# Both feed-forwards in five token blocks instead of six, with a ring of 1536 places

## The chip, the cores and the metric

The kernel runs on one core of a Trainium2 chip. The core has a matrix engine (TensorE, PE in the profile, its weight loads PEld), a vector engine (DVE), an activation engine (ACT), a general engine (POOL) and an engine that here only issues DMA transfers (SP). On-chip data lies in SBUF; matmul results lie in eight PSUM banks of 512 fp32 columns each. The metric is the device time of one execution in microseconds. Before the change it was 864.6 us, the median of 3 runs (862.94 to 866.23).

## The reference, cut to what matters

```
x = dilated/windowed attention(q, k, v)   # 4 batches, 8 heads, 576 tokens, head size 64
                                          # heads 0-3: the last 32 keys; heads 4-7: every 4th of the last 128
x = x as 2304 tokens x 512
h = x @ moe_w_in                          # 512 -> 2048
x = (h * cos(h)) @ moe_w_out              # 2048 -> 512
h = max(x @ w1, x @ w2, x @ w3)           # 512 -> 768, three times
y = h @ w_out                             # 768 -> 512
```

Inputs and output are fp32.

## The kernel before, in words

**Precision.** The big products are made of three passes in the fp32r type: every operand is kept as a rounded half "hi" and a rest half "lo", and hi·hi, lo·hi and hi·lo are added in PSUM (`PASSES`). So one 128 x 128 block of weights costs three matmuls per block of tokens. A matmul has the weights as its stationary operand (128 columns, loaded anew for each matmul) and the tokens of the current block as its moving operand (320 to 512 columns).

**The attention** is cut into 48 units: a unit is one batch, one pair of heads and 192 queries. Per unit PE makes the scores (L254, or L257 for the first 12 units), DVE adds the mask and takes the maximum (L261, into a tile `e`), ACT takes the exponential (L203), DVE or POOL normalizes (L293), PE transposes (L301), ACT or DVE copies (`pt`, L138) and PE multiplies with the values (L312). DVE then writes hi and lo of the result into the **ring** (L326, L328), the SBUF store from which the first feed-forward reads its tokens. In the ring of 1152 places a batch lies at place `b % 2 * 576`.

**The first feed-forward (FF1)** walks over six blocks of tokens (`BLOCKS1`, 512, 320, 320, 448, 320 and 384 tokens). A block has 16 steps, one for each 128 of the 2048 hidden columns. A step has 12 matmuls `h` (L342), the evaluation of h·cos(h) on DVE and ACT (kk L358 or L356, r L362, clamp L365, sine L203, product L374, halves L138/L134 and L376), and 12 matmuls that add the step of three steps before (`LAG = 3`) to four accumulator banks (L385). The `h` results take turns in two PSUM banks, so the `h` of step s+2 waits until the product of step s (L374) has read its bank. At the end of a block the four accumulators are copied to tiles `o` (L398, L400) and sent to a DRAM tensor x1d. These tiles have a pool of their own with two buffers (`osp`).

**The order of attention and FF1.** The 12 units of batch 0 come first, with the loads of the first weights. The units that a later block needs are run during the block before it: `plan[t]` lists the units that block t needs in addition, and `enter` spreads them over the first `LAST[t]` steps of the block before. With the six blocks these are 12 units ahead of FF1, and then 10, 2, 12, 8, 4 and 0 units during blocks 0 to 5. The pieces of a unit are put between the matmul groups of a step. Block 0 also converts the 32 FF1 weight tiles from 64-bit words to fp32 (ACT L175, DVE L181 and L184) and splits them into halves (L138, L194).

**The second feed-forward (FF2)** also has six blocks (`BLOCKS2`, 512, 320, 320, 512, 320, 320) with 6 steps each; a step has 36 matmuls (L342) for the three products, two maxima on DVE, and 12 accumulating matmuls (L385). Its tokens come back from x1d by batch (`x1_raw`) and are split into the ring (`x1_split`, L415, L416); the first batch is split during the last FF1 block. Its 24 weight tiles are loaded during the last FF1 block, as FF1 weight slots come free, and converted during that block and the first FF2 block.

**What sets the order.** The framework places the instructions of each engine with a scheduler of its own, by priority (about the order of the program text) and by estimated times; the order in the text is not always the order on the engine. All DMA transfers are issued in order by SP. `RUNS` is the number of SBUF tiles for loaded q/k/v groups: the load for unit n + RUNS is issued when unit n is done (`att_done`). The pool `tmp` (4 buffers) holds kk, r and the maxima, `sp` (4) holds the tiles `e`.

Of the kernel before, what the change touches and what calls it, by code (L numbers as in the profile page):

```python
# [8 lines left out]
F32 = mybir.dt.float32  # L9
F32R = mybir.dt.float32r  # L10
# [8 lines left out]
B, H, S, D = 4, 8, 576, 64  # L19
# [10 lines left out]
NC = DM // 128  # L30
NF1 = FF1 // 128
NF2 = FF2 // 128

BLOCKS1 = [512, 320, 320, 448, 320, 384]
BLOCKS2 = [512, 320, 320, 512, 320, 320]
TB = max(BLOCKS1 + BLOCKS2)
NBT = len(BLOCKS1)
RING = 2 * S
LAG = 3
RUNS = 6  # L40
KEYS = 2 * QB + WIN
START = (3, 6, 7)
STARTS1 = [sum(BLOCKS1[:n]) for n in range(len(BLOCKS1))]
STARTS2 = [sum(BLOCKS2[:n]) for n in range(len(BLOCKS2))]
WSLOTS = 2 * NF1

INV2PI = 1.0 / (2.0 * math.pi)
# [15 lines left out]
}  # L63


LAST = (13, 7, 10, 7, 8)
GROUP = (2, 1, 1, 1, 1, 1)

START_WEIGHTS = (0, 0, 2, 1, 0, 0, 0, 1, 0, 0, 1, 0, 1, 0, 1)
STEP_WEIGHTS = (  # L70
# [9 lines left out]
def token_runs(pair, i):  # L80

    if pair < 2:
        return [(0, 2 * QB, 2 * QB * i, 1)]
    out = []
    p, end = 2 * QB * i, 2 * QB * (i + 1)
    while p < end:
        r, t = divmod(p, S // 4)
        n = min(end - p, S // 4 - t)
        out.append((p - 2 * QB * i, n, 4 * t + r, 4))
        p += n  # L90
    return out
# [3 lines left out]
def body(  # L95
# [11 lines left out]
    nc = tc.nc  # L107
    pool = lambda name, bufs, **kw: ctx.enter_context(tc.tile_pool(name=name, bufs=bufs, **kw))
# [2 lines left out]
    wx = pool("wx", 2)  # L111
    xp = pool("xp", 1)
    ip = pool("ip", RUNS)
    tmp = pool("tmp", 4)
    gp = pool("gp", 2)
    sp = pool("sp", 4)
    ptp = pool("ptp", 2)
    smp = pool("smp", 8)
    osp = pool("osp", 2)
    drp = pool("drp", 1, space=bass.MemoryType.DRAM)  # L120
    ps = pool("ps", 1, space=PSUM)

# [23 lines left out]
    bank = [ps.tile([128, 512], F32, name=f"bank{n}") for n in range(8)]  # L146
    acc = bank[:4]
    h_bank = bank[4:6]
    a_bank = bank[6:]
# [156 lines left out]
    def att_out(u):  # L306
        b, p, i = u
        pt = st.pop(u)
        vs = given.pop(u)
        o = bank[places.pop(u)[1]]  # L310
        for j, h in HEADS:
            nc.tensor.matmul(  # L312
                o[64 * h : 64 * h + 64, j * QB : (j + 1) * QB],
                vs[j][2][:, 64 * h : 64 * h + 64],
                pt[:, 2 * j + h, :],
                start=True,
                stop=True,
            )
        x = ring[p]
        at = b % 2 * S  # L320
        parts = [
            (o[:, o0 : o0 + n], slice(at + t0, at + t0 + step * (n - 1) + 1, step))
            for o0, n, t0, step in token_runs(p, i)
        ]
        for ov, cols in parts:
            nc.vector.tensor_copy(x[:, 0, cols], ov)  # L326
        for ov, cols in parts:
            nc.vector.tensor_tensor(  # L328
                out=x[:, 1, cols], in0=ov, in1=x[:, 0, cols].bitcast(F32), op=ALU.subtract
            )  # L330


    g = {}
    PASSES = ((0, 0), (1, 0), (0, 1))

    def h_chunks(hv, w, t0, n_tok):

        c0 = t0 % RING

        def chunk(n, c):  # L340
            for j, (a, x) in enumerate(PASSES):
                nc.tensor.matmul(  # L342
                    hv,
                    w[:, a, 128 * c : 128 * c + 128],
                    ring[c][:, x, c0 : c0 + n_tok],
                    start=n == 0 and j == 0,
                    stop=n == NC - 1 and j == 2,
                )

        return chunk  # L350
# [30 lines left out]
    def acc_chunk(dst, t0, first, last, w, gt, dm):  # L381
        n_tok = gt.shape[-1]
        a_dm = acc[dm][:, :n_tok]
        for n, (a, x) in enumerate(PASSES):
            nc.tensor.matmul(  # L385
                a_dm,
                w[:, a, 128 * dm : 128 * dm + 128],
                gt[:, x, :],
                start=first and n == 0,
                stop=last and n == 2,  # L390
            )
        if last:
            if dst is x1d:
                o = osp.tile([128, TB], F32, tag="o", name="o")[:, :n_tok]
            else:
                o = ip.tile([128, TB], F32, tag="qkv", name="o")[:, :n_tok]
            if dm % 2:
                nc.vector.tensor_copy(o, a_dm)  # L398
            else:
                nc.scalar.copy(o, a_dm)  # L400
            nc.sync.dma_start(out=dst[dm, :, t0 : t0 + n_tok], in_=o)
# [1 line left out]

    x1raw = {}

    def x1_raw(b, c):
        raw = ip.tile([128, S], F32, tag="qkv", name="x1raw")
        nc.sync.dma_start(out=raw, in_=x1d[c, :, b * S : (b + 1) * S])
        x1raw[b, c] = raw

    def x1_split(b, c):
        raw = x1raw.pop((b, c))
        at = b % 2 * S
        hi, lo = (ring[c][:, x, at : at + S] for x in range(2))
        nc.scalar.copy(hi, raw)  # L415
        nc.vector.tensor_tensor(out=lo, in0=raw, in1=hi.bitcast(F32), op=ALU.subtract)  # L416

# [2 lines left out]
    def ff2_h(s):  # L420
        t, f = divmod(s, NF2)
        m = None
        for j in range(3):
            hv = (h_bank + a_bank)[flip[0] % 4][:, : BLOCKS2[t]]
            flip[0] += 1
            chunk = h_chunks(hv, halves[(j, f)], STARTS2[t], BLOCKS2[t])
            for n in range(NC):
                chunk(n, n)
            if j == 0:
                m = tmp.tile([128, TB], F32, tag="r", name="mx")[:, : BLOCKS2[t]]  # L430
                nc.vector.tensor_copy(m, hv)  # L431
            else:
                nc.vector.tensor_tensor(out=m, in0=hv, in1=m, op=ALU.max)  # L433
        gt = gp.tile([128, 2, TB], F32R, tag="g", name="gt")[:, :, : BLOCKS2[t]]
        nc.scalar.copy(gt[:, 0, :], m)  # L435
        nc.vector.tensor_tensor(
            out=gt[:, 1, :], in0=m, in1=gt[:, 0, :].bitcast(F32), op=ALU.subtract
        )
        g[s] = gt

    def ff2_acc(s):
        t, f = divmod(s, NF2)
        for dm in range(NC):
            acc_chunk(outT, STARTS2[t], f == 0, f == NF2 - 1, halves[("o", f)], g[s], dm)


    list1 = [("in", f) for f in range(LAG)]
# [34 lines left out]
    for t in range(NBT):  # L482
        us = []
        for b in range(B):
            n_tok = min(STARTS1[t] + BLOCKS1[t] - b * S, S)
            if n_tok > 0:
                us += units(b, dil, range(3)) + units(b, plain, range(-(-n_tok // (2 * QB))))
        plan.append([u for u in us if u not in sum(plan, [])])
# [47 lines left out]
    for s in range(NS + LAG):  # L536
# [16 lines left out]
        t, f = divmod(s, NF1)  # L553
        if s < NS:

            hv = (bank[3] if s == 2 else h_bank[(s + (s > 2)) % 2])[:, : BLOCKS1[t]]
            hc = h_chunks(hv, halves[("in", f)], STARTS1[t], BLOCKS1[t])
            chunks += [("h", n, c) for n, c in enumerate((2, 3, 0, 1))]
        if s >= LAG:
            chunks += [("a", dm, 0) for dm in range(NC)]  # L560
# [1 line left out]
        for j, (kind, x, c) in enumerate(chunks):  # L562
            if kind == "h":
                hc(x, c)
                if x == NC - 1:
                    hvs[s] = hv
                    ff1_reduce(s, hv)
            else:
                t0, f0 = divmod(s - LAG, NF1)
                acc_chunk(x1d, STARTS1[t0], f0 == 0, f0 == NF1 - 1, halves[("out", f0)], g[s - LAG], x)  # L570
            while done < len(pieces) and done * len(chunks) < (j + 1) * len(pieces):
                do, u = pieces[done]
                do(u)
                done += 1
            if j == 1:
                if s >= 1 and s - 1 < NS:
                    ff1_g(s - 1)
            if s < NF1:
                weights(STEP_WEIGHTS[s].count(j), WSLOTS)
# [3 lines left out]
            att_norm(to_norm, zt, tensor("norm"))  # L583
            to_out += to_norm
        to_norm = []
        if len(to_exp) >= GROUP[min(t, NBT - 1)] or (to_exp and s % NF1 >= LAST[min(t, 4)]):
            zt = att_exp(to_exp)
            to_norm, to_exp = to_exp, []
        k = s - (NS - NF1) - LAG - 1
# [6 lines left out]
            x1_split(0, k // 2 - 2)  # L596


    N2 = len(BLOCKS2) * NF2
    x1_at = {0: 1}  # L600
    for b in (2, 3):

        t = min(t for t in range(len(BLOCKS2)) if STARTS2[t] >= (b - 1) * S)
        x1_at[t * NF2] = b
    todo = []
    for s in range(N2 + 1):
        if s in x1_at:
            b = x1_at[s]
            todo += [(b, c) for c in range(NC)]
            for bc in todo[:2]:  # L610
                x1_raw(*bc)
        while at[3] < min(len(order), len(list1) + 4 * (s + 2)):
            weight_loads(1, len(order))
            weights(1, len(order))
        if s < N2:
            ff2_h(s)
        if s:
            ff2_acc(s - 1)
        if todo:
            x1_split(*todo.pop(0))  # L620
            if len(todo) >= 2:
                x1_raw(*todo[1])
# [79 lines left out]
```

## Time and profile before

| | |
|---|---|
| median of 3 runs | 864.6 us |
| the profiled execution | 862.63 us |
| its span, first to last instruction | 860.9 us |
| PE busy | 826.0 us, 96% |
| DVE busy | 541.2 us, 63% |
| ACT busy | 342.2 us, 40% |
| POOL busy | 107.0 us, 12% |
| granted TensorE clock, mean | 0.983 |

The busy time of PE is a union of records that overlap, since matmuls are pipelined: a matmul record lasts about 0.3 to 0.4 us, while the next one starts 0.15 to 0.23 us after it. What a matmul costs is therefore read from the distance between starts, or from the chain of waits, which gives a run of matmuls and the time that it took. A stage's cost is read from a table of windows whose edges are the first `h` matmul of each block.

### The profile page before, as it was taken

How to read it: one execution, taken by the hardware profiler on the slowest of the kernel's cores; microseconds unless marked ns; L12 is line 12 of the kernel's file. 1: busy time of each engine (PE TensorE's matmuls, PEld its weight loads, DVE VectorE, ACT ScalarE, POOL GpSimd, SP SyncE). 2: the span in 40 equal slices, each digit the busy share in tenths (PEclk: the TensorE clock that was granted, in tenths of full speed). 3: DMA queues.
4: the chain of work that ended last, by engine and by line, in shares of the span. 5: the costliest groups of instructions: out<-in, count | busy, mean ns of one | idle time of the engine just before them, and what ended most of it. 6: DMA issues, size and time to landing. Idle time of an engine off the chain costs nothing.

```text
span 860.9 us, 13231 instructions
## 1 busy us (share of the span) xinstructions
PE 826.0 (96%) x5030; PEld 734.5 (85%) x5030; DVE 541.2 (63%) x1466; ACT 342.2 (40%) x794; POOL 107.0 (12%) x104
## 2 busy tenths in 40 slices
PE   7858979999999999999999999999999999999998
PEld 6636657789988898889989999888899998889998
DVE  5989996566687877875676899982233333223232
ACT  6977857343278827832452445400011111001001
POOL 1654453110000000000000011210000000000000
PEclk9978999999999999999999999999999999999999
DMA  9972100110011211120110387100020201001000
GB/s 352 410 290 102 49 26 23 49 66 18 1 50 51 73 53 47 50 59 1 36 50 14 116 253 231 65 19 0 1 77 1 87 1 58 1 1 50 1 32 31
DMA packets 24400, 62.31 MB, mean 72 GB/s; under 512 B 2704, under 2 KB 7440, under 8 KB 24336
## 3 DMA queue, kind: packets, MB, share of 16 engines
q1 hardware_dynamic: 24336, 61.47, 20.9%
q8 instruction: 39, 0.64, 0.3%
q14 instruction: 25, 0.20, 0.1%
HBM read 52.02 MB, written 9.44 MB: 71 GB/s over the span
## 4 chain that ended last, share of the span: by engine, by line
PE 75%; DVE 11%; DMA 7%; ACT 3%; issue 2%; POOL 1%; SPq 0%; ACTq 0%; POOLq 0%; DVEq 0%
PE bank L342 42%; PE bank L385 26%; PE bank L254 3%; DMA w<-in_w_out 2%; DMA w<-in_w_in 2%; PE bank L312 2%; DVE wx L181 2%; DVE wx L184 2%; DMA x1d<-o 1%; PE bank L301 1%; ACT e L203 1%; DVE r L365 1%; DVE r L362 1%; DVE r L374 1%; DMA qkv<-in_qkv 1%
## 5 line engine op out<-in xcount | busy, mean ns | idle before, releaser
L342 PE MATMUL bank<-ring,w 128*128 128x320 f32 (+3 forms) x2448 | 471.1, 342 | 8.7 <-DVE r L374 7.7
L342 PEld LDWEIGHTS bank<-ring,w 128*128 128x128 f32 x2448 | 401.7, 189 | 42.1 <-DVE r L374 9.1
L385 PE MATMUL bank<-gt,w 128*128 128x320 f32 (+3 forms) x1584 | 314.0, 341 | 2.0 <-DVE gt L376 1.3
L385 PEld LDWEIGHTS bank<-gt,w 128*128 128x128 f32 x1584 | 262.0, 189 | 25.5 <-DVE gt L376 2.0
L203 ACT ACTIVATE r<-r,hpi 128x320 f32<-128x320 f32 (+3 forms) x96 | 59.2, 617 | 142.3 <-DVE r L365 141.9
L435 ACT CAST gt<-mx 128x320 fp32r<-128x320 f32 (+1 forms) x36 | 18.5, 514 | 226.5 <-DVE mx L433 226.5
L433 DVE TENSOR_TENSOR mx<-bank,mx 128x320 f32<-128x320 f32 (+1 forms) x72 | 40.1, 557 | 94.3 <-PE bank L342 94.3
L203 ACT ACT_TABLE_LOAD x58 | 74.4, 1283 | 18.5 <-DVE r L365 15.1
L203 ACT ACTIVATE e<-e,m 96x128 f32<-96x128 f32 x192 | 74.8, 391 | 7.1 <-DVE m L261 6.7
L194 POOL TENSOR_TENSOR w<-wx,w 128x512 fp32r<-128x512 f32 x44 | 60.7, 1388 | 123.2 <-DVE w L138 63.6
L374 DVE TENSOR_TENSOR r<-bank,r 128x320 f32<-128x320 f32 (+3 forms) x96 | 52.9, 552 | 23.7 <-ACT r L203 23.5
L431 DVE COPY mx<-bank 128x320 f32<-128x320 f32 (+1 forms) x36 | 20.1, 558 | 72.5 <-PE bank L342 72.5
L362 DVE SCALAR_TENSOR_TENSOR r<-kk,bank 128x320 f32<-128x320 int32 (+3 forms) x96 | 52.7, 549 | 9.6 <-ACT kk L356 7.9
L358 DVE TENSOR_SCALAR kk<-bank 128x320 int32<-128x320 f32 (+2 forms) x80 | 42.0, 525 | 26.5 <-PE bank L342 26.4
L261 DVE CUSTOM_DVE_ANT_0 e<-bank,cs 96x128 f32<-96x128 f32 x192 | 44.9, 282 | 14.8 <-PE bank L257 8.6
L134 POOL TENSOR_SCALAR gt<-r 128x320 fp32r<-128x320 f32 (+2 forms) x32 | 16.1, 503 | 288.1 <-PE bank L385 224.7
L376 DVE TENSOR_TENSOR gt<-r,gt 128x320 fp32r<-128x320 f32 (+3 forms) x81 | 42.7, 528 | 13.7 <-POOL gt L134 10.5
L184 DVE SCALAR_TENSOR_TENSOR wx<-w,wx 128x512 int32<-128x512 int32 x56 | 46.2, 828 | 0.3
L175 ACT ACTIVATE w<-w 128x512 f32<-128x512 f32 x56 | 36.4, 671 | 14.5 <-DMA w<-in_w 14.2
L254 PE MATMUL bank<-qkv 64*96 64x128 f32 x288 | 36.7, 299 | 3.7 <-DVE m L261 2.6
L365 DVE TENSOR_SCALAR r<-r 128x320 f32<-128x320 f32 (+3 forms) x96 | 39.4, 410 | 1.3
L254 PEld LDWEIGHTS bank<-qkv 64*96 64x96 f32 x288 | 25.3, 165 | 17.4 <-issue 6.3
(37 smaller groups left out, 509.4 us busy)
## 6 DMA issues: line engine op xcount, KB each, us to landing
qkv<-in_qkv SPq DMA_DIRECT2D x36, 336.0 KB, 2.9
w<-in_w SPq DMA_DIRECT2D x18, 512.0 KB, 4.5
w<-in_w_in SPq DMA_DIRECT2D x16, 512.0 KB, 9.4
w<-in_w_out SPq DMA_DIRECT2D x16, 512.0 KB, 10.0
qkv<-in_qkv SPq DMA_DIRECT2D x12, 432.0 KB, 9.3
x1raw<-x1d SPq DMA_DIRECT2D x16, 288.0 KB, 3.2
w<-in_w_o SPq DMA_DIRECT2D x6, 512.0 KB, 4.3
outT<-o SPq DMA_DIRECT2D x16, 160.0 KB, 1.8
```

Of the source, the lines that this page charges most:

```text
L184: nc.vector.scalar_tensor_tensor(out=x, in0=low, scalar=29, in1=x, op0=ALU.logical_shift_right, op1=ALU.bitwise_or)
L194: tensor("w_lo").tensor_tensor(out=w[:, 1, :], in0=x, in1=w[:, 0, :].bitcast(F32), op=ALU.subtract)
L203: last_table.append(nc.scalar.activation(*args, **kw).ins)
L254: nc.tensor.matmul(sv, q[rows], k[rows], start=True, stop=True)
L261: nc.vector.tensor_tensor_reduce(out=e[:, 2 * j + h, :], in0=places_of[j, h], in1=mask[:, kind, :], scale=-1.0 / math.sqrt(D), scalar=3e38 ...
L342: nc.tensor.matmul(hv, w[:, a, 128 * c : 128 * c + 128], ring[c][:, x, c0 : c0 + n_tok], start=n == 0 and j == 0, stop=n == NC - 1 and j == 2,
L358: nc.vector.tensor_scalar(out=kk.bitcast(I32), in0=hv, scalar1=INV2PI, scalar2=0.25, op0=ALU.mult, op1=ALU.add)
L362: nc.vector.scalar_tensor_tensor(out=r, in0=kk.bitcast(I32), scalar=-2.0 * math.pi, in1=hv, op0=ALU.mult, op1=ALU.add)
L365: nc.vector.tensor_scalar(out=r, in0=r, scalar1=ARG_HI, scalar2=ARG_LO, op0=ALU.min, op1=ALU.max)
L374: nc.vector.tensor_tensor(out=r, in0=hv, in1=r, op=ALU.mult)
L376: tensor("g_lo").tensor_tensor(out=gt[:, 1, :], in0=r, in1=gt[:, 0, :].bitcast(F32), op=ALU.subtract)
L385: nc.tensor.matmul(a_dm, w[:, a, 128 * dm : 128 * dm + 128], gt[:, x, :], start=first and n == 0, stop=last and n == 2,)
```

## The change

Both feed-forwards use one list of blocks, `BLOCKS = [512, 512, 512, 512, 256]`. A block of FF1 has 16 steps as before and a block of FF2 has 6. The ring has 1536 places, the first three blocks; a token t lies at place t % 1536, so a unit of batch 2 or 3 can cross the ring's end, and its copy into the ring is then cut in two (`parts`). FF2 no longer loads x1 by batch: it loads and splits it by block (`x1_raw(t, c)`, `x1_split(t, c)`), block t + 1 in the first steps of block t, at the places `AT2`. The plan of units follows from the blocks: 12 ahead of FF1, and then 12, 10, 12, 2 and 0 units during blocks 0 to 4, spread by the new `LAST`. The buffers: `tmp` has 5 (was 4) and also takes the tiles `o` of FF1, whose pool of two goes; `sp` has 3 (was 4), `RUNS` is 5 (was 6).

```diff
-BLOCKS1 = [512, 320, 320, 448, 320, 384]
-BLOCKS2 = [512, 320, 320, 512, 320, 320]
-RING = 2 * S
+BLOCKS = [512, 512, 512, 512, 256]
+RING = sum(BLOCKS[:3])
+AT2 = [RING - TB, 0, TB, RING - TB, 0]
-RUNS = 6
+RUNS = 5
-LAST = (13, 7, 10, 7, 8)
-GROUP = (2, 1, 1, 1, 1, 1)
+LAST = (13, 10, 12, 8)
+GROUP = (2, 1, 1, 1, 1)
...
-    tmp = pool("tmp", 4)
+    tmp = pool("tmp", 5)
-    sp = pool("sp", 4)
+    sp = pool("sp", 3)
-    osp = pool("osp", 2)
...
-        at = b % 2 * S
-        parts = [
-            (o[:, o0 : o0 + n], slice(at + t0, at + t0 + step * (n - 1) + 1, step))
-            for o0, n, t0, step in token_runs(p, i)
-        ]
+        parts = []
+        for o0, n, t0, step in token_runs(p, i):
+
+            while n:
+                at = (b * S + t0) % RING
+                k = min(n, (RING - at + step - 1) // step)
+                parts.append((o[:, o0 : o0 + k], slice(at, at + step * (k - 1) + 1, step)))
+                o0, n, t0 = o0 + k, n - k, t0 + step * k
...
-                o = osp.tile([128, TB], F32, tag="o", name="o")[:, :n_tok]
+                o = tmp.tile([128, TB], F32, tag="r", name="o")[:, :n_tok]
...
-    def x1_raw(b, c):
-        raw = ip.tile([128, S], F32, tag="qkv", name="x1raw")
-        nc.sync.dma_start(out=raw, in_=x1d[c, :, b * S : (b + 1) * S])
-        x1raw[b, c] = raw
+    def x1_raw(t, c):
+        raw = ip.tile([128, TB], F32, tag="qkv", name="x1raw")[:, : BLOCKS[t]]
+        nc.sync.dma_start(out=raw, in_=x1d[c, :, STARTS[t] : STARTS[t] + BLOCKS[t]])
+        x1raw[t, c] = raw
...
-            n_tok = min(STARTS1[t] + BLOCKS1[t] - b * S, S)
+            n_tok = min(STARTS[t] + BLOCKS[t] - b * S, S)
...
     for s in range(N2 + 1):
-        if s in x1_at:
-            b = x1_at[s]
-            todo += [(b, c) for c in range(NC)]
-            for bc in todo[:2]:
-                x1_raw(*bc)
+
+        if s % NF2 == 0 and s // NF2 + 1 < NBT:
+            todo += [(s // NF2 + 1, c) for c in range(NC)]
+            for key in todo[:2]:
+                x1_raw(*key)
```

## Rows read from the trace of the kernel before

**Rows 1.** The page: engines (section 1), then the chain of waits by engine.
```profile
PE 826.0 (96%) x5030; PEld 734.5 (85%) x5030; DVE 541.2 (63%) x1466; ACT 342.2 (40%) x794; POOL 107.0 (12%) x104
PE 75%; DVE 11%; DMA 7%; ACT 3%; issue 2%; POOL 1%; SPq 0%; ACTq 0%; POOLq 0%; DVEq 0%
```

**Rows 2.** Windows, edges at each FF1 block's first matmul and FF2's first two blocks.
```profile
core 0: us, PE busy (x) PEld busy (x) DVE busy (x) ACT busy (x) POOL busy (x), PEclk, DMA share, GB/s
22.74:171.08 148.34, 127.10 (x696) 93.44 (x695) 121.19 (x337) 103.49 (x256) 69.05 (x51) 0.92 0.36 134
171.08:234.76 63.68, 63.40 (x426) 59.98 (x425) 42.37 (x110) 21.01 (x45) 5.15 (x9) 1.00 0.09 29
234.76:320.13 85.37, 85.12 (x627) 74.82 (x626) 67.57 (x258) 58.06 (x143) 3.68 (x8) 1.00 0.19 57
320.13:412.79 92.66, 92.02 (x547) 79.73 (x546) 68.10 (x204) 46.81 (x105) 4.76 (x8) 1.00 0.12 37
412.79:480.63 67.84, 67.54 (x466) 63.41 (x465) 48.40 (x139) 32.29 (x70) 3.81 (x8) 1.00 0.11 33
480.63:557.52 76.89, 73.99 (x423) 71.57 (x422) 74.40 (x154) 36.87 (x66) 11.59 (x9) 1.00 0.57 180
557.52:620.12 62.60, 62.60 (x278) 51.84 (x277) 31.26 (x50) 4.21 (x7) 4.97 (x4) 1.00 0.04 13
```

**Rows 3.** The page, costliest groups: the two feed-forward matmul lines and L342's weight loads.
```profile
L342 PE MATMUL bank<-ring,w 128*128 128x320 f32 (+3 forms) x2448 | 471.1, 342 | 8.7 <-DVE r L374 7.7
L342 PEld LDWEIGHTS bank<-ring,w 128*128 128x128 f32 x2448 | 401.7, 189 | 42.1 <-DVE r L374 9.1
L385 PE MATMUL bank<-gt,w 128*128 128x320 f32 (+3 forms) x1584 | 314.0, 341 | 2.0 <-DVE gt L376 1.3
```

**Rows 4.** Chain of waits in time order: matmul runs at 512, 320, 448 columns; attention.
```profile
160.03 0.34 PE bank L301 x4
163.15 0.48 PE bank L312 x8
168.66 2.72 PE bank L385 x12
171.81 0.61 PE bank L254 x8
205.14 1.76 PE bank L385 x12
391.20 2.43 PE bank L385 x12
```

**Rows 5.** Timeline: start, duration; two groups at 384 columns; two weight loads after a wait.
```profile
513.51 2.24 PE L342 MATMUL bank<-ring,w 128*128 128x384 f32 x12
515.59 2.24 PE L385 MATMUL bank<-gt,w 128*128 128x384 f32 x12
...
27.49 0.30 PEld L342 LDWEIGHTS bank<-ring,w 128*128 128x128 f32 x2
```

**Rows 6.** DVE groups by shape (busy us, mean ns | idle before): L376 at three widths.
```profile
L376 DVE TENSOR_TENSOR gt<-r,gt 128x320 fp32r<-128x320 f32 x48 | 23.3, 485 | 8.3 <-POOL gt L134 6.7 <-ACT gt L138 1.6
L376 DVE TENSOR_TENSOR gt<-r,gt 128x448 fp32r<-128x448 f32 x16 | 10.0, 623 | 3.8 <-POOL gt L134 2.9 <-ACT gt L138 0.7
```

**Rows 7.** DVE groups by shape in the last FF1 block's window.
```profile
L181 DVE TENSOR_SCALAR wx<-w 128x512 int32<-128x512 int32 x18 | 12.6, 708 | 0.0
L358 DVE TENSOR_SCALAR kk<-bank 128x384 int32<-128x384 f32 x16 | 8.8, 548 | 0.9 <-PE bank L342 0.9
L365 DVE TENSOR_SCALAR r<-r 128x384 f32<-128x384 f32 x16 | 5.6, 350 | 0.0
```

**Rows 8.** Waits, whole span: who waited for whom, us in total, times, longest.
```profile
ACT o L400 <- DMA x1d<-o: 7.9, 3, 2.7
DVE o L398 <- DMA x1d<-o: 3.3, 4, 1.4
```

**Rows 9.** SP's waits, then its timeline at FF1 block 3's start.
```profile
SPq L217 <- PE bank L312: 241.9, 23, 49.9
...
336.59 0.33 SPq L217 DMA_DIRECT2D qkv<-in_qkv  x1
337.12 5.94 SPq L401 DMA_DIRECT2D x1d<-o  x4
344.69 0.33 SPq L217 DMA_DIRECT2D qkv<-in_qkv  x1
```

**Rows 10.** PE timeline in the start: scores (L257) and transposes (L301) of first units.
```profile
17.05 1.11 PE L257 MATMUL bank<-qkv 128*96 128x128 f32 x8
19.72 0.55 PE L301 MATMUL bank<-cs,e 96*128 96x96 f32 x4 [1.55 <-POOL e L293]
```

More of the change, by code (lines that the diff above doesn't have):

```diff
@@ L32 @@
 NF2 = FF2 // 128
-BLOCKS1 = [512, 320, 320, 448, 320, 384]
-BLOCKS2 = [512, 320, 320, 512, 320, 320]
-TB = max(BLOCKS1 + BLOCKS2)
-NBT = len(BLOCKS1)
-RING = 2 * S
+BLOCKS = [512, 512, 512, 512, 256]
+STARTS = [sum(BLOCKS[:n]) for n in range(len(BLOCKS))]
+TB = max(BLOCKS)
+NBT = len(BLOCKS)
+RING = sum(BLOCKS[:3])
+AT2 = [RING - TB, 0, TB, RING - TB, 0]
 LAG = 3
-RUNS = 6
+RUNS = 5
 KEYS = 2 * QB + WIN
 START = (3, 6, 7)
-STARTS1 = [sum(BLOCKS1[:n]) for n in range(len(BLOCKS1))]
-STARTS2 = [sum(BLOCKS2[:n]) for n in range(len(BLOCKS2))]
 WSLOTS = 2 * NF1
@@ L334, in body, with h_chunks @@
     PASSES = ((0, 0), (1, 0), (0, 1))
-    def h_chunks(hv, w, t0, n_tok):
-        c0 = t0 % RING
+    def h_chunks(hv, w, c0, n_tok):
         def chunk(n, c):
@@ L404, in body, with x1_split @@
     x1raw = {}
-    def x1_raw(b, c):
-        raw = ip.tile([128, S], F32, tag="qkv", name="x1raw")
-        nc.sync.dma_start(out=raw, in_=x1d[c, :, b * S : (b + 1) * S])
-        x1raw[b, c] = raw
[L411 to L414, printed above, removed]
+    def x1_raw(t, c):
+        raw = ip.tile([128, TB], F32, tag="qkv", name="x1raw")[:, : BLOCKS[t]]
+        nc.sync.dma_start(out=raw, in_=x1d[c, :, STARTS[t] : STARTS[t] + BLOCKS[t]])
+        x1raw[t, c] = raw
+    def x1_split(t, c):
+        raw = x1raw.pop((t, c))
+        hi, lo = (ring[c][:, x, AT2[t] : AT2[t] + BLOCKS[t]] for x in range(2))
         nc.scalar.copy(hi, raw)
@@ L423, in ff2_h @@
         for j in range(3):
-            hv = (h_bank + a_bank)[flip[0] % 4][:, : BLOCKS2[t]]
+            hv = (h_bank + a_bank)[flip[0] % 4][:, : BLOCKS[t]]
             flip[0] += 1
-            chunk = h_chunks(hv, halves[(j, f)], STARTS2[t], BLOCKS2[t])
+            chunk = h_chunks(hv, halves[(j, f)], AT2[t], BLOCKS[t])
             for n in range(NC):
@@ L429, in ff2_h @@
             if j == 0:
-                m = tmp.tile([128, TB], F32, tag="r", name="mx")[:, : BLOCKS2[t]]
+                m = tmp.tile([128, TB], F32, tag="r", name="mx")[:, : BLOCKS[t]]
                 nc.vector.tensor_copy(m, hv)
@@ L433, in ff2_h @@
                 nc.vector.tensor_tensor(out=m, in0=hv, in1=m, op=ALU.max)
-        gt = gp.tile([128, 2, TB], F32R, tag="g", name="gt")[:, :, : BLOCKS2[t]]
+        gt = gp.tile([128, 2, TB], F32R, tag="g", name="gt")[:, :, : BLOCKS[t]]
         nc.scalar.copy(gt[:, 0, :], m)
@@ L443, in ff2_acc @@
         for dm in range(NC):
-            acc_chunk(outT, STARTS2[t], f == 0, f == NF2 - 1, halves[("o", f)], g[s], dm)
+            acc_chunk(outT, STARTS[t], f == 0, f == NF2 - 1, halves[("o", f)], g[s], dm)
     list1 = [("in", f) for f in range(LAG)]
@@ L554, in body @@
         if s < NS:
-            hv = (bank[3] if s == 2 else h_bank[(s + (s > 2)) % 2])[:, : BLOCKS1[t]]
-            hc = h_chunks(hv, halves[("in", f)], STARTS1[t], BLOCKS1[t])
+            hv = (bank[3] if s == 2 else h_bank[(s + (s > 2)) % 2])[:, : BLOCKS[t]]
+            hc = h_chunks(hv, halves[("in", f)], STARTS[t] % RING, BLOCKS[t])
             chunks += [("h", n, c) for n, c in enumerate((2, 3, 0, 1))]
@@ L569, in body @@
                 t0, f0 = divmod(s - LAG, NF1)
-                acc_chunk(x1d, STARTS1[t0], f0 == 0, f0 == NF1 - 1, halves[("out", f0)], g[s - LAG], x)
+                acc_chunk(x1d, STARTS[t0], f0 == 0, f0 == NF1 - 1, halves[("out", f0)], g[s - LAG], x)
             while done < len(pieces) and done * len(chunks) < (j + 1) * len(pieces):
@@ L585, in body @@
         to_norm = []
-        if len(to_exp) >= GROUP[min(t, NBT - 1)] or (to_exp and s % NF1 >= LAST[min(t, 4)]):
+        if len(to_exp) >= GROUP[min(t, NBT - 1)] or (to_exp and s % NF1 >= LAST[min(t, len(LAST) - 1)]):
             zt = att_exp(to_exp)
@@ L596, in body @@
             x1_split(0, k // 2 - 2)
[L599 to L604, printed above, removed]
+    N2 = NBT * NF2
     todo = []
     for s in range(N2 + 1):
-        if s in x1_at:
-            b = x1_at[s]
-            todo += [(b, c) for c in range(NC)]
-            for bc in todo[:2]:
-                x1_raw(*bc)
+        if s % NF2 == 0 and s // NF2 + 1 < NBT:
+            todo += [(s // NF2 + 1, c) for c in range(NC)]
+            for key in todo[:2]:
+                x1_raw(*key)
         while at[3] < min(len(order), len(list1) + 4 * (s + 2)):
```

## The prediction

> **What bounds the kernel now.** I read the engines first: PE is busy for 96% of the span, the next engine for 63%, and the chain that ended last lies on PE for 75% of it [rows 1]. Then I read windows, one for each FF1 block [rows 2]. After 171 us PE is busy nearly all of each window (63.40 of 63.68 us, 85.12 of 85.37 us), at full granted clock; in block 0 it is busy for 127.10 of 148.34 us at a mean clock of 0.92, and DVE for 121.19 us. In the last FF1 block DVE is as full as PE (74.40 and 73.99 of 76.89 us). So most of the kernel is a stream of matmuls. What counts is their number, their spacing and what is put between them; only block 0 and the last FF1 block have a second engine near its limit.
>
> The spacing comes from the chain of waits, which has runs of 12 matmuls [rows 4]: 2.72 us at 512 columns (226.7 ns each), 1.76 us at 320 (146.7 ns), 2.43 us at 448 (202.5 ns). At 384 two groups of 12 start 2.08 us apart (173.3 ns) [rows 5]. Between 320 and 512 columns 192 columns cost 80 ns, so 0.4167 ns a column, and 13.3 ns are left over at either width. At 384 this gives 173.3, as read; at 448 it gives 200, 2.5 below the row.
>
> **1. Fewer matmuls.** The kernel has 2448 + 1584 = 4032 feed-forward matmuls [rows 3]: six blocks of 16 x 24 + 6 x 48 = 672. Five blocks make 3360. The columns are the same. So 672 x 13.3 ns = 9.0 us go, if the 256-wide matmuls keep to the line at 106.7 + 13.3 = 120 ns. No row has a width below 320. From above, their spacing is bounded by that of 320 columns, 146.7 ns, which would add 672 x 26.7 ns = 17.9 us; below, 106.7 ns of columns remain, which would give another 9 us. I take 120: the widths from 320 to 512 show no bend towards either end.
>
> The Trainium skill (TensorE: Matmul & The Clock Gate, Back-to-back issue gap) puts an isolated matmul at N / 2.4 + 2.5 ns. By that the fixed part would be 2.5 ns, this term 1.7 us instead of 9.0, and the whole sum -4.2 us. The trace does not agree: it has 13.3 ns at two widths.
>
> **2. Two more attention units in block 0 (12 instead of 10).** The window of block 0 is 148.34 us; its 192 `h` and 156 accumulating matmuls at 226.7 ns are 78.9 us. The other 69.4 us are 10 units, the end of the first 12 units and the conversion of the weights. A unit's bare matmuls on PE take 0.61 + 0.34 + 0.48 = 1.43 us [rows 4]; that is the lower end. The upper end is all of the 69.4 us shared by 10 units, 6.9 us. I take 2.5 us, a little over the rate of the later blocks (step 3), since PE is the fuller engine here too but DVE is close behind. That is +5 us (2.9 to 13.9).
>
> **3. 24 instead of 26 units in the middle blocks, between wider matmul groups.** Blocks 1 to 4 take 63.68 + 85.37 + 92.66 + 67.84 = 309.55 us [rows 2]. Their matmuls, 384 each: 3 x 56.3 + 77.8 us, and 2.9 us more because the first 36 accumulating ones belong to the 512-wide block 0; 249.7 us. That leaves 59.9 us for 26 units, with all stalls. Block by block (each with 36 accumulating matmuls of the block before) it is 4.5 us for 2 units, 29.0 for 12 (2.42 each), 16.9 for 8 (2.11 each, the 448-wide block) and 9.5 for 4. Wider groups give the other engines more time between two pieces of a unit, and the 448-wide block is the row nearest to 512: I take 2.1 us. 24 x 2.1 = 50.4 us, so -9.5 us. At 2.42 it is -1.8; at the bare 1.43 it would be -25.6.
>
> **4. The last FF1 block, 256 instead of 384 wide.** Now PE has 384 x 173.3 ns and 36 x 146.7 ns there, 71.8 us of the 76.89, so 5.1 us are lost. The first FF2 block loses nothing: 276 x 226.7 ns = 62.6 us. Its DVE is busy for only 31.26 us. DVE's FF1 work per step is four operations of 548 ns and one of 350 [rows 7], 40.7 us over 16 steps; the other 33.7 us are mostly 18 conversions of FF2 weights and the split of x1. From 485 ns at 320 and 623 at 448 [rows 6] I put a 256-wide operation at 420 ns and the clamp at 290, as an estimate, so 31.5 us. PE needs 384 x 120 + 36 x 226.7 ns = 54.2 us, in which DVE has 22.7 us left. So 11 us of conversions move to the first FF2 block, which has room for them. But a step now lasts 2.9 us, and the `h` banks come free later in proportion; I take 7 us lost instead of 5.1, +2. The ends: nothing lost, -5.1; or all 33.7 us stay in this block, which then lasts 31.5 + 33.7 + the 2.5 that DVE was idle = 67.7 us, 13.5 lost, +8.4.
>
> **5. Buffers, ring and x1.** I cost them at nothing. Two of the four `o` copies now wait for the landing of the others (7.9 us on ACT and 3.3 on DVE in the whole span, at most 2.7 at once [rows 8]), while PE goes on with the next `h`; five `tmp` buffers end that, and hand the wait to the kk and r that follow. With three `e` tiles the scores of a unit can no longer be masked before the third one before it is transposed: in the start the scores of a unit ran at 17.05 and that transposition at 19.72 [rows 10], so up to 2.7 us, once; the loop behind it is in that order anyway. Five q/k/v tiles leave a load three wide steps ahead of its use. The split at the ring's end adds two short DVE copies in six units, in blocks where DVE has a quarter of its time free. x1 by block moves the same bytes, in stages where PE alone is full. Ends for all of it: 0 to +2.7.
>
> **The sum**, against the profiled execution's 862.63 us (1.7 us over its span): -9.0 + 5 - 9.5 + 2 = -11.5, so 851.1. The median shown is 864.6, 0.23% above that execution, which makes 853 us.
>
> **The rivals.**
> - *The middle blocks gain nothing per unit* (2.42 us, as where 12 units share 16 steps now): 7.7 us less gain, 861. For it: block 2 in the change also has 12 units. Against it: its steps were 320 wide.
> - *Block 0 is bound by DVE, ACT and POOL together*, and a unit costs 6.9 us there: 8.9 us more, 862. For it: 121.19 and 103.49 us busy of 148.34. Against: most of the 69.4 us is weight conversion, which stays.
> - *DVE holds the last FF1 block* with all its conversions: 6.4 us more than forecast, 859.5.
> - *The other side: the weight load becomes the bound in the 256-wide block.* A load of 128 columns lasts 189 ns on average [rows 3], longer than 120. Where a matmul is as short as 120 ns the load of the next may not fit under it. If the spacing stays at the 146.7 ns of 320 columns, 17.9 us come on top: 871 us, slower. It decides from about 137 ns (11.5 us over 672 matmuls) for no gain. For it: no matmul with such a load is shown less than 146.7 ns after the one before. Against it: loads already overlap by 42 ns there, and two loads of the same shape after a wait of PE take 0.30 us together, 190 ns of it the second one's own, so they began 110 ns apart [rows 5].
> - *`o` tiles block `tmp`.* They leave by SP, which waits 241.9 us in all for q/k/v tiles to come free [rows 9]. If a load that waits for the next unit's output stood ahead of the four sends, the r of the next steps would wait a step of 7.3 us, at the starts of blocks 1, 2 and 3: +22, 875. Against it: in the row the load stands ahead and the sends followed within 0.5 us.
> - *More gain*: units at 1.8 us and block 0 at +3 give -20.7, 844.
>
> **How the numbers follow.** Forecast 0.48 (848 to 858), more gain 0.12, DVE in the last block 0.09, middle blocks 0.10, block 0 0.10, weight loads 0.06, `o` tiles 0.05. 0.5% (4.3 us, about what a measurement can tell from no change) puts the borders at 860.3 and 868.9. Faster: 0.48 + 0.12 + 0.09, and 0.06 of the two cases that lie close to the border (861 and 862), 0.75. Same: the other 0.14 of those and 0.01 of the weight loads, in a mild form, 0.15. Slower: the rest of the weight loads and the `o` tiles, 0.10. The range 844 to 866 leaves out the slow rivals and a little of the fast end.
>
> **What would show it.** Right: 3360 feed-forward matmuls; 12 matmuls of 256 columns in 1.44 us; block 0's window about 153 us; blocks 1, 2 and 3 near 108, 112 and 92 us; the last FF1 window near 61 us with DVE full in it; FF2 with no idle PE. Wrong: runs of 256-wide matmuls above 1.6 us per 12; a block 0 window above 160 us; PE waiting for r or kk right after a block's end, with x1d as the releaser; PE waits for L374 of many microseconds in the last FF1 block.

## The result, and the profile after

The changed kernel takes 852.9 us (median of 4 runs, 851.57 to 854.55) against 863.8 us before (4 runs, 862.94 to 866.23): a ratio of 0.9872, with a 95% interval of 0.9852 to 0.9892. The profiled execution took 854.55 us, 852.8 of them its span; it is the slowest of the four. Executions of one program differ with the clock granted in block 0: over the runs of the kernel before beside the experiments, a mean clock of 0.978 went with 866.2 to 868.3 us, one of 0.986 with 862.1 to 865.3. A block 0 window is therefore good to some 3 us (e1 and e5 below run the same block 0 and differ by 2.3), while the windows behind it, at a clock of 1.00 (2.4 GHz), repeat within 0.7 us, most within 0.4.

The windows of the changed kernel (start and end, length, busy us of PE, PEld, DVE, ACT and POOL, clock, DMA), with edges at the first matmul of each FF1 block, at FF2 and at its second block, answer to [rows 2]:

```profile
23.50:179.20 155.70, 133.59 (x736) 97.49 (x735) 126.47 (x362) 110.01 (x277) 69.12 (x51) 0.91 0.36 129
179.20:289.98 110.77, 110.77 (x586) 84.25 (x585) 80.35 (x246) 58.64 (x126) 6.31 (x9) 1.00 0.14 41
289.98:402.06 112.09, 112.09 (x626) 84.66 (x625) 86.75 (x265) 69.36 (x150) 5.15 (x8) 1.00 0.16 49
402.06:494.27 92.21, 92.21 (x426) 74.06 (x425) 59.63 (x116) 28.42 (x51) 5.01 (x8) 1.00 0.09 28
494.27:551.13 56.85, 55.51 (x421) 52.82 (x420) 52.91 (x132) 32.80 (x65) 8.45 (x6) 1.00 0.67 241
551.13:614.15 63.03, 63.03 (x279) 51.84 (x278) 40.55 (x67) 4.07 (x7) 9.99 (x6) 1.00 0.03 9
614.15:852.80 238.65, 234.95 (x1166) 198.93 (x1164) 71.40 (x116) 23.85 (x44) 0.00 (x0) 1.00 0.08 29
```

| stage, us of the span | before | forecast | after |
|---|---|---|---|
| start to the end of block 0 | 171.08 | 176.1 | 179.20 |
| the middle blocks | 309.55 (4) | 311.6 (3) | 315.07 (3) |
| the last FF1 block | 76.89 | 61.2 | 56.85 |
| FF2 and the end | 303.4 | 299.5 | 301.7 |
| span | 860.9 | 848.4 | 852.8 |

The forecast column is put together from the prediction's terms: 171.08 + 5; 3 x 384 x 226.7 ns + 50.4 us; 54.2 + 7; 303.4 less 288 x 13.3 ns. It is 1 us below the prediction's own sum (849.4), since some matmuls cross the windows' edges. Every stage but the last FF1 block came out longer than forecast, that one 4.4 us shorter.

The chain of waits in FF2 (start, us, what), against [rows 4]:

```profile
765.19 2.79 PE bank L386 x12
767.99 8.18 PE bank L343 x36
...
830.41 4.31 PE bank L343 x36
834.72 1.43 PE bank L386 x12
```

At 256 columns 12 accumulating matmuls (L386) take 1.43 us and 36 of the products (L343) 4.31, both 119 to 120 ns each, as forecast. At 512 columns the products are where they were (8.18 us for 36, 227 ns), but 12 accumulating ones take 2.79 us, not 2.72: the same matmul in the same stage, 6 ns longer (6.1 by the starts in the trace), with nothing else on the chain. No step of the prediction had that, and the experiments began there.

### The profile page after: what moved, and what is told of

Read it like the earlier page. It is cut to its first block, busy times and chain, and to the rows that moved or that the text cites. A ratio compares the mean times of both kernels' runs of the same rounds, so it can differ in the third digit from the quotient of the medians.

```text
span 852.8 us, 11770 instructions
## 1 busy us (share of the span) xinstructions
PE 820.5 (96%) x4358; PEld 659.7 (77%) x4358; DVE 531.0 (62%) x1376; ACT 341.3 (40%) x770; POOL 108.0 (13%) x96
## 4 chain that ended last, share of the span: by engine, by line
PE 83%; DVE 6%; DMA 6%; issue 2%; POOL 2%; ACT 1%; SPq 0%; POOLq 0%; ACTq 0%
PE bank L343 46%; PE bank L386 30%; DMA w<-in_w_in 3%; PE bank L253 3%; DMA qkv<-in_qkv 2%; PE bank L311 2%; PE bank L300 1%; POOL w L193 1%; DVE wx L183 1%; DVE r L366 1%; DVE wx L180 1%; DVE r L363 1%; DVE gt L377 1%; DMA w<-in_w_o 1%; DVE r L375 1%
## 5 line engine op out<-in xcount | busy, mean ns | idle before, releaser
L343 PE MATMUL bank<-ring,w 128*128 128x512 f32 (+1 forms) x2040 | 465.6, 376 | 9.7 <-DVE r L375 7.1
L343 PEld LDWEIGHTS bank<-ring,w 128*128 128x128 f32 x2040 | 353.7, 190 | 79.6 <-DVE r L375 8.4
L386 PE MATMUL bank<-gt,w 128*128 128x512 f32 (+1 forms) x1320 | 307.2, 377 | 0.6 <-DVE gt L377 0.6
L386 PEld LDWEIGHTS bank<-gt,w 128*128 128x128 f32 x1320 | 229.3, 189 | 48.4 <-DVE gt L377 0.8
L202 ACT ACTIVATE r<-r,hpi 128x512 f32<-128x512 f32 (+1 forms) x80 | 54.5, 681 | 115.0 <-DVE r L366 114.6
L433 DVE TENSOR_TENSOR mx<-bank,mx 128x512 f32<-128x512 f32 (+1 forms) x60 | 38.2, 637 | 88.6 <-PE bank L343 88.6
L375 DVE TENSOR_TENSOR r<-bank,r 128x512 f32<-128x512 f32 (+1 forms) x80 | 50.4, 632 | 21.9 <-ACT r L202 21.7
L359 DVE TENSOR_SCALAR kk<-bank 128x512 int32<-128x512 f32 (+1 forms) x64 | 39.7, 621 | 28.9 <-PE bank L343 28.7
L363 DVE SCALAR_TENSOR_TENSOR r<-kk,bank 128x512 f32<-128x512 int32 (+1 forms) x80 | 50.3, 629 | 8.3 <-ACT kk L357 7.2
L377 DVE TENSOR_TENSOR gt<-r,gt 128x512 fp32r<-128x512 f32 (+1 forms) x65 | 42.8, 658 | 14.9 <-POOL gt L133 10.9
L366 DVE TENSOR_SCALAR r<-r 128x512 f32<-128x512 f32 (+1 forms) x80 | 37.6, 470 | 0.9
```

What stands on the lines that cost most here:

```text
L202: last_table.append(nc.scalar.activation(*args, **kw).ins)
L343: nc.tensor.matmul(hv, w[:, a, 128 * c : 128 * c + 128], ring[c][:, x, c0 : c0 + n_tok], start=n == 0 and j == 0, stop=n == NC - 1 and j == 2,
L359: nc.vector.tensor_scalar(out=kk.bitcast(I32), in0=hv, scalar1=INV2PI, scalar2=0.25, op0=ALU.mult, op1=ALU.add)
L363: nc.vector.scalar_tensor_tensor(out=r, in0=kk.bitcast(I32), scalar=-2.0 * math.pi, in1=hv, op0=ALU.mult, op1=ALU.add)
L366: nc.vector.tensor_scalar(out=r, in0=r, scalar1=ARG_HI, scalar2=ARG_LO, op0=ALU.min, op1=ALU.max)
L375: nc.vector.tensor_tensor(out=r, in0=hv, in1=r, op=ALU.mult)
```

## The experiments

The kernel before ran beside each, on the same chip. Medians are compared by ratio; stages by windows or the chain.

**e1, gt moved.** The tiles gt are what L386 reads as its moving operand. Between the weights and gt lie the ring, the q/k/v tiles and tmp. All their sizes are multiples of 256 bytes per partition but that of a q/k/v tile, 672 x 4 = 2688 = 10.5 x 256. With six of them gt stands a multiple of 256 bytes away from the weights, with five it is 128 off.

```diff
+    gp = pool("gp", 2)
     ip = pool("ip", RUNS)
     tmp = pool("tmp", 5)
-    gp = pool("gp", 2)
```

> The changed kernel with one line moved: the pool of the g tiles (gt) is allocated right behind the ring instead of behind tmp. Every engine's instructions and their order stay the same, only SBUF addresses differ. Theory A (the address of gt slows the 512-wide accumulating matmuls, which read it): in the second feed-forward a run of 12 of them takes 2.72 us again instead of 2.79, 1056 such matmuls give back about 6 us, and the time falls from 852.9 to about 847 us. Rival (the 6 ns come from the other tokens' widths or from another engine's traffic): still 2.79 us per 12 and 853 us.

Measured: 848.4 us, ratio 0.9814 (0.9794 to 0.9833). The chain in FF2, and the windows of blocks 0 to 3, the last FF1 block and FF2:

```profile
573.38 2.72 PE bank L386 x12
576.10 8.16 PE bank L343 x36
```

```profile
23.50:175.91 152.41, 131.26 (x735) 96.11 (x734) 126.24 (x359) 109.62 (x275) 68.08 (x51) 0.93 0.36 132
175.91:286.08 110.17, 110.17 (x586) 84.23 (x585) 80.28 (x246) 58.63 (x126) 6.24 (x9) 1.00 0.14 42
286.08:397.67 111.59, 111.59 (x626) 84.60 (x625) 86.81 (x265) 69.44 (x150) 5.10 (x8) 1.00 0.17 49
397.67:488.67 91.00, 91.00 (x426) 74.06 (x425) 59.32 (x116) 28.44 (x51) 4.97 (x8) 1.00 0.09 28
488.67:545.85 57.18, 55.90 (x421) 53.11 (x420) 52.80 (x132) 33.17 (x65) 8.44 (x6) 1.00 0.67 240
545.85:845.50 299.65, 296.07 (x1443) 250.98 (x1441) 111.60 (x183) 27.92 (x51) 9.95 (x6) 1.00 0.07 25
```

Every instruction is the same and in the same order, and the accumulating matmuls are back at 2.72 us. The middle blocks give 2.3 us and FF2 2.0; block 0 is 3.3 us shorter, of which its 156 such matmuls explain 1 us and the clock (0.93, not 0.91) can be the rest: e5 below has the same instructions there, in the same order and with gt in the same place, and took 2.3 us longer than e1 at a clock of 0.90. The row of e5's block 0:

```profile
23.73:178.40 154.67, 133.34 (x735) 97.60 (x734) 126.16 (x358) 109.50 (x275) 67.96 (x51) 0.90 0.35 129
```

The median falls by 4.5 us (5.0 by the ratios, 0.9872 and 0.9814), less than the 6 expected.

**e2, e9, e10 and e11, the place of gt in the kernel before.** A pad of 128, 64 or 256 bytes ahead of gt, and in e11 one of 128 bytes ahead of the weights, so that weights, ring and gt move together:

```diff
+    pad = pool("padp", 1).tile([128, 32], F32, name="pad")   # 64 bytes: 16, 256 bytes: 64
+    nc.gpsimd.memset(pad, 0.0)
     gp = pool("gp", 2)                                        # e11: ahead of wp = pool("wp", 1)
```

> The kernel before with a pad of 128 bytes per partition ahead of the g tiles (one memset of it on GpSimd at the start), all else the same. Theory A (it is gt's place modulo 256 bytes against the weights' that counts): runs of 12 accumulating matmuls at 512 columns in the second feed-forward go from 2.72 to about 2.79 us, and the whole is 1 to 4 us slower than before (865 to 868 us), depending on what 320 columns do. Rival: 2.72 us, no change (864 us).

> The kernel before with a pad of 64 bytes per partition ahead of gt. The pad of 128 bytes (e2) made the 512-wide accumulating matmuls of the second feed-forward 233 ns apart instead of 226.7. Theory F (gt's place modulo 256 bytes counts, and only the half-way place is bad): 226.7 ns or some value between. Rival (any shift off the common place costs the same): 233 ns, 2.79 us per 12.

> The kernel before with a pad of 256 bytes per partition ahead of gt. Theory F (the place counts modulo 256 bytes): 226.7 ns, 2.72 us per 12, as without a pad. Rival (it counts modulo more, or the pad's memset is what disturbs): 2.79 us.

> The kernel before with the pad of 128 bytes ahead of the weights instead of ahead of gt, so that weights, ring and gt all move by 128 bytes; gt then has the same address as in e2, where its matmuls were 233 ns apart. Theory G (the distance of gt from the weights counts): 2.72 us per 12 accumulating matmuls at 512 columns in the second feed-forward. Rival (gt's own address counts): 2.79 us, and the matmuls that read the ring slow down too, from 8.16 to about 8.4 us per 36.

The chain of each in its first FF2 block; e2, then e9, e10 and e11:

```profile
585.34 2.79 PE bank L387 x12
588.13 8.18 PE bank L344 x36
```

```profile
585.36 2.76 PE bank L387 x12
588.13 8.21 PE bank L344 x36
```

```profile
586.25 2.72 PE bank L387 x12
588.97 8.16 PE bank L344 x36
```

```profile
585.22 2.72 PE bank L387 x12
587.94 8.16 PE bank L344 x36
```

128 bytes off: 2.79 us. 64 off: 2.76, but there the 36 products behind them take 8.21 us, so a step of both lasts 10.97 us in either case. 256 off: 2.72, and 10.88 for the step. And with gt at the very address of e2 but the weights moved along: 2.72 and 10.88. (e9 to e11 were executed once each; within the block these rows repeat from step to step.) So gt's own address does not count, but its distance from what lies ahead of it, modulo 256 bytes as far as these four places show; both places off the multiple that were tried cost the same 0.09 us a step. Of what lies ahead, an accumulating matmul reads only the weights. The ring and the q/k/v tiles, however, moved with the weights in e11, so the runs do not tell them from the weights; `tmp` is out, since in e1 gt stands 128 bytes off it. On the whole of the kernel before the effect is not to be seen (e2: ratio 1.0003, 0.9986 to 1.002), since only 336 of its 1584 accumulating matmuls are 512 wide (2 us) and the 320-wide ones take 1.76 us per 12 as before. After the change 1056 are 512 wide. Of the 1 to 4 us expected of e2 the interval leaves 1.7 at most.

**e5 and e6, other blocks** (both with gt as in e1):

```diff
-BLOCKS = [512, 512, 512, 512, 256]
+BLOCKS = [512, 512, 512, 384, 384]    # e5
+BLOCKS = [384] * 6                    # e6; AT2, LAST and GROUP to match
```

> The changed kernel with gt right behind the ring (as in e1), and the blocks 512, 512, 512, 384, 384: again five blocks and 3360 matmuls, but no 256-wide block. Theory C (only the number of matmuls counts, 13.3 ns each): the second feed-forward takes as long as in e1 (299.7 us) within 1 us, and the whole 848 to 850 us, since the last block has 384 columns again and loses about 2 us more to DVE. Rival (256 columns carry a hidden cost of their own): faster than e1, 845 us or less. Other rival (blocks of 512 are worth more than the count says): 852 us or more.

> As e1, but six blocks of 384, so 4032 matmuls again, with a ring of 1152 places and the buffers of the change. Theory C: the second feed-forward takes 3.8 us longer than in e1 (288 more matmuls at 13.3 ns), 303.5 us as before the change, and the whole 9 us more than e1, 857 us, if the attention keeps its price of 2.15 us a unit in the middle blocks. Rival (what was gained came from wider groups between the attention pieces, not from the count): the second feed-forward unchanged against e1, the middle blocks dearer per unit.

Measured: e5 850.95 us, ratio 0.9859 (0.9843 to 0.9874), just above the 848 to 850 expected; e6 872.8 us, ratio 1.0112 (1.0094 to 1.013), slower than before. FF2 in e5; then blocks 1 to 4 and FF2 in e6:

```profile
550.09:849.70 299.61, 296.11 (x1442) 262.08 (x1440) 100.89 (x168) 27.85 (x51) 6.74 (x4) 1.00 0.08 26
```

```profile
158.32:490.59 332.27, 331.63 (x2098) 302.38 (x2097) 244.98 (x751) 177.98 (x391) 17.91 (x33) 1.00 0.14 40
...
567.51:870.80 303.29, 299.82 (x1730) 299.50 (x1728) 104.75 (x194) 31.06 (x63) 4.20 (x3) 1.00 0.08 28
```

In FF2, where there is nothing but these matmuls, the count decides to within 0.2 us: 299.61 and 299.65 us for five blocks of either kind, 303.29 for six of 384 and 303.4 for the six of before. e6 as a whole missed its 857 us. 4 x 384 matmuls of 173.3 ns are 266.2 us of its middle blocks, so 66.1 us went to the 28 units that run there, 2.36 each; in e1 it is 312.76 - 261.2 = 51.6 us for 24 units, 2.15 each. These 14.5 us, with 9 for the matmuls, make nearly all of its 25.3 us span over e1. Of the 14.5, four units more at e1's price are 8.6, and the higher price of all 28 is 5.9: the units and the matmuls weigh about the same here. Block 0 runs four units fewer in e6, but at a clock of 0.85; what that gave back is not shown.

**e4, two units earlier.** In the kernel before, block 1's two units run in block 0.

```diff
+    plan[1], plan[2] = plan[1] + plan[2], []
     runs = sum(plan, [])
```

> The kernel before, with the two attention units that block 1 runs moved into block 0 (12 units there, none in block 1), as the change has it. Theory B (two more units in block 0 cost the 8 us that the changed kernel's block 0 shows): block 0's window grows by about 8 us, block 1's shrinks by 4.5, 867 us in all. Rival (the 2.5 us per unit of the prediction are right and the rest comes with three e tiles or the other order): +5 - 4.5, 864.5 us.

Measured: 859.55 us, ratio 0.9934 (0.9911 to 0.9958). Blocks 0 and 1:

```profile
23.24:173.00 149.76, 130.41 (x736) 95.45 (x735) 125.04 (x361) 110.08 (x276) 69.87 (x51) 0.93 0.38 136
173.00:232.25 59.26, 59.26 (x386) 57.74 (x385) 36.93 (x82) 12.49 (x25) 5.16 (x9) 1.00 0.05 19
```

Block 0 ends 1.9 us later than before, block 1 is 4.4 us shorter. With ten units block 0 ended between 171.1 and 173.0 us in the kernel before, e2 and e9 to e12, so at a like clock two units more cost it some 2 us at most. Both expectations, 5 and 8, were too high.

**e8, four more units early**, in e1: four units of batch 2 run in block 0, 16 there, one in each step.

```diff
+    due = [list(us) for us in plan]
+    early = units(2, plain, range(2))
+    plan[1] = plan[1] + early
+    plan[2] = [u for u in plan[2] if u not in early]
...
-LAST = (13, 10, 12, 8)
+LAST = (16, 10, 12, 8)
```

> As e1, with four plain attention units of batch 2 moved from block 1 into block 0 (16 there, one a step, and 6 in block 1). In e4 two more units cost block 0 about 1.9 us and gave 4.4 back in block 1. Theory E (PE waits in block 0 anyway, so a unit costs about 1 us there and 2.15 in the blocks behind it): block 0 grows by about 4 us, block 1 shrinks by 8.6, 844 us. Rival (with 16 units DVE, ACT and POOL are the bound in block 0): block 0 grows by 8 us or more, no gain, 848 us or more.

Measured: 846.8 us, ratio 0.9815 (0.98 to 0.983), the same as e1 within the intervals. Blocks 0 and 1:

```profile
23.29:183.70 160.41, 138.85 (x779) 100.42 (x778) 133.73 (x399) 116.25 (x295) 67.93 (x51) 0.91 0.35 125
183.70:287.01 103.31, 103.31 (x542) 80.48 (x541) 73.67 (x203) 46.83 (x103) 6.42 (x9) 1.00 0.15 44
```

Block 0 grows by 8.0 us, block 1 shrinks by 6.9. Theory E fell: PE sat idle for 21.6 us of block 0 (160.41 - 138.85), as in e1 (152.41 - 131.26 = 21.2), so the four units did not go into its free time but added 7.6 us of PE's own. The clock was lower as well (0.91, not 0.93), and what keeps PE waiting there was not found.

**e3, e12 and e7, the buffers.** e3 is the kernel before with five q/k/v tiles, the `o` tiles in a `tmp` of five, and gt behind the ring; e12 has only the part with the `o` tiles. e7 is e1 with four `e` tiles and four `tmp` tiles.

```diff
-RUNS = 6                                  # e3 alone
+RUNS = 5
-    tmp = pool("tmp", 4)                  # e3 and e12
+    tmp = pool("tmp", 5)
-    osp = pool("osp", 2)
...
-    tmp = pool("tmp", 5)                  # e7
-    sp = pool("sp", 3)
+    tmp = pool("tmp", 4)
+    sp = pool("sp", 4)
```

> The kernel before with the blocks of before but the buffers of the change, as far as its order allows: five q/k/v tiles, five tmp tiles that also take the o tiles, no pool for o; four e tiles as before, and gt at a place like the ring's. The prediction (the buffers cost nothing): 864 us, within 1.5. Rival (o tiles hold up r and kk at the block starts): 2 to 6 us at each of five starts, 870 us or more.

> The kernel before with only one part of e3: five tmp tiles that also take the o tiles, and no pool for o; six q/k/v tiles as before, gt's place as before modulo 256. e3 was 0.45% faster than before, against the prediction's nothing; its window of FF1 block 2 was 2.6 us shorter. Theory H (the o copies that waited for the landing of earlier ones were what cost): the same gain here, about 861 us, block 2's window near 82.7 us. Rival (the five q/k/v tiles, through the order of the loads and units, made it): 864.5 us, block 2's window 85.4 us.

> As e1, but with four e tiles (as before the change) and four tmp tiles instead of three and five. Block 0 and the start ended at 175.9 us in e1, against 173.0 in the kernel before with the same 12 units in block 0 (e4). Theory D (the third e tile's wait costs these 3 us): the end of block 0 falls to about 173 us and the whole by 2 to 3 us. Rival (the place of weights and attention on the engines, or the granted clock, makes the difference): within 1.5 us of e1.

Measured: e3 861.5 us, ratio 0.9955 (0.9935 to 0.9976); e12 862.8 us, 0.9998 (0.9982 to 1.0015); e7 849.5 us, 0.985 (0.9828 to 0.9873), no better than e1. FF1 block 2 in e3, in e12, then block 0 and the last FF1 block in e7:

```profile
239.27:322.00 82.73, 82.41 (x627) 73.13 (x626) 67.42 (x258) 58.01 (x142) 3.69 (x8) 1.00 0.20 59
```

```profile
235.37:320.56 85.19, 84.88 (x627) 74.41 (x626) 67.42 (x258) 58.06 (x142) 3.66 (x8) 1.00 0.20 58
```

```profile
23.23:174.19 150.96, 131.36 (x735) 95.73 (x734) 121.65 (x358) 109.41 (x274) 70.07 (x51) 0.93 0.36 133
...
487.48:545.40 57.92, 54.67 (x410) 51.74 (x408) 51.11 (x128) 32.29 (x62) 9.89 (x6) 1.00 0.69 237
```

The `o` tiles in `tmp` are worth nothing that the medians show, either way: theory H fell. What made e3 faster is thus left to the five q/k/v tiles or the place of gt beside the ring. The matmuls of e3 and e12 come in another order from block 0 on, and block 2 of the old blocks is 2.6 us shorter than before. With gt alone moved (e2, e9, e10, e11) block 2 lasts 85.4 us at each of its places, so the five tiles are the likelier cause; they were not tested alone. With four `e` tiles block 0 ends 1.7 us earlier than in e1, one execution of each. What comes behind it takes 2.9 us longer (846.7 - 174.19 against 845.5 - 175.91); that the fifth `tmp` tile is missed there is likely, but was not tested alone. Nothing is gained.

## Why the prediction was right, point by point

The total was right, 853 against 852.9 us. Of its five terms two held (1 and 3) and three did not, with errors in both directions.

1. *Fewer matmuls, -9.0 us.* The mechanism and the size held: 120 ns at 256 columns, and 3.7 us between five and six blocks of FF2 in e1, e5 and e6, where 288 x 13.3 ns = 3.8 us were forecast. The rival in which the weight load bounds the 256-wide matmuls is out. What was missed is on the other side of the same term: 1056 accumulating matmuls became 6 ns longer, 6.4 us by their number, of which e1 gave 4.5 to 5.0 back.
2. *Two units more in block 0, +5 us.* Too high for the units (some 2 us at most in e4), too low for the stage, which ended 8.1 us later in the profile. Of that, 1 us is the place of gt; 1.7 us went with three `e` tiles in e7, a price that the prediction had bounded at 2.7 and then left at nothing, though one pair of executions does not show it beyond doubt. The granted clock can have a share as large: e1 and e5, with the same block 0, lie 2.3 us apart. The prediction's upper end also took for the units' time what the clock costs: its 78.9 us of matmuls are at the spacing of the full clock, in a window granted 0.92.
3. *24 units instead of 26, at 2.1 us.* After the change it is (315.07 - 261.2) / 24 = 2.24 us; less the 576 accumulating matmuls at 6.1 ns (3.5 us) it is 2.10, and 2.15 in e1. The step held in its mean, but units are not alike: in e8 four units of heads 0 to 3 fewer made block 1 6.9 us shorter, 1.7 each, and the six of heads 4 to 7 that stayed cost (103.31 - 87.05) / 6 = 2.7. That the wider group between two pieces is what lowers the price was argued from one row and is not shown. For it: the same mix of 12 units cost 2.42 each at 320 columns and (111.59 - 87.05) / 12 = 2.05 at 512 in e1. Against it: in another order they cost 2.20 at 320 in e3, and e6 has 2.36 at 384, above the mean of 59.9 / 26 = 2.30 before.
4. *The last FF1 block, +2 us.* Here the step failed in sign: 56.85 - 54.2 = 2.6 us are lost, where 5.1 were and 7 were forecast. I had expected the shorter step to run into DVE more often; all the waits of `h` for the product (L375) in this window come to 1.5 us. DVE's other work gave way instead. Its groups by shape in this window (busy us, mean ns) show 14 and not 18 conversions of FF2 weights begun, at 486 ns each and not 708 [rows 7]. Three of the four FF1 operations take 409 to 413 ns where 420 were estimated, the fourth (L377) 562:

```profile
L180 DVE TENSOR_SCALAR wx<-w 128x512 int32<-128x512 int32 x14 | 6.7, 486 | 1.0 <-ACT w L174 1.0
L359 DVE TENSOR_SCALAR kk<-bank 128x256 int32<-128x256 f32 x16 | 6.6, 411 | 0.0
L377 DVE TENSOR_TENSOR gt<-r,gt 128x256 fp32r<-128x256 f32 x16 | 9.0, 562 | 0.1
```

   The first FF2 block took the conversions in: DVE is busy for 40.55 us there, against 31.26 before [rows 2], and PE loses nothing to it. The split of x1 (L416) went the other way, into the block ahead, which the prediction had not foreseen. DVE's time for it in the last FF1 block, before and after:

```profile
480.63:557.52 76.89, 4.50 (x6) 1.00 0.57 180
494.27:551.13 56.86, 0.00 (x0) 1.00 0.67 241
```

5. *Buffers, at nothing.* This is the step that was wrong, twice over. The count of q/k/v tiles moved gt against the weights, which cost what e1 gave back, 4.5 to 5.0 us; and nearly the same buffers (four `e` tiles) at the old blocks, with gt in a good place, gain 0.45% (e3). If that gain is there at the new blocks too, which no run shows, the two nearly cancel; the errors of steps 2 and 4 have opposite signs as well. Between the two profiled executions the span fell by 8.1 us and not by 11.5. That the total came out within 0.1 us is luck in its last few microseconds.

The other rivals: no kk or r waited for x1d (the wait of the `o` copies [rows 8] is gone; in e12, at the old blocks, one kk waited 1.0 us in its place and the median stayed), the middle blocks kept their gain, and DVE did not hold the last block.

The best versions are e1 and e8, 848.4 and 846.8 us, not told apart: the change with gt's pool declared behind the ring's, 1.9% below the kernel before.

## What to carry to other kernels

Where PE is the bound, cost a change of block size by a stage that holds nothing but matmuls: columns times the slope, plus a fixed part per matmul, read from two widths. Then ask of every other stage what stands between the matmuls: here the attention units in the middle blocks took 59.9 us before, 51.6 in e1 and 66.1 in e6, differences as large as that of the matmuls (9 us). Moving units ahead is no gain by itself: two moved out of block 1 helped the kernel before (e4), four more did nothing (e8). And a change of a buffer's count moves every tile allocated behind it: compare the time of one unchanged instruction before and after, and where it differs with the same neighbours, move the tile before looking for a wait.

## What the runs showed of the hardware

The spacing of the accumulating fp32r matmuls depends on where their moving operand lies against the weights (or against the ring and the q/k/v tiles, which these runs do not tell apart from them). At a distance of a multiple of 256 bytes per partition it is 226.7 ns at 512 columns (2.72 us per 12), at 64 bytes off 230, at 128 off 233; at 64 bytes off the products that follow slow down too, so a step of 12 and 36 takes 10.97 us at either place against 10.88. Moving weights, ring and gt together changes nothing (e11). At 256 columns the sign is the other way and small: 1.43 us per 12 after the change, 1.44 in the chain of e1:

```profile
815.95 1.44 PE bank L386 x12
```

At 320 columns nothing is seen (1.76 us per 12 in e2 too). The Trainium skill (SBUF — State Buffer, Who interferes with whom) gives PE two independent read ports, for the moving operand and the weight load, and says that PE never waits on anyone. These runs show a dependence that this leaves out, 6 ns a matmul by the place of the moving operand; whether two of PE's own reads meet there is not shown.
